# The tail of a Fourier-mixing and GEGLU kernel: the next to last drain copied into buffers of its own ahead of the last chunk's halves, and drain additions spread two per unit

## Chip, cores and metric

The kernel runs on one core of one Trainium2 chip. The metric is the device time of one execution in microseconds (us); the number to compare is the median of several runs. Times inside the program are taken from one profiled execution and counted from the start of its span.

## What is computed

```python
a = jnp.einsum("bsd,ed->bse", x, dft_hid_re)     # x: the input, layer-normed
b = jnp.einsum("bsd,ed->bse", x, dft_hid_im)
y = jnp.einsum("ts,bse->bte", dft_seq_re, a) - jnp.einsum("ts,bse->bte", dft_seq_im, b)
...
h = x + _A_ref(_layernorm(x, axis=-1), ...)      # the mixing above
...
g = jnp.einsum("bsd,df->bsf", x, w_gate)         # x: h, layer-normed
u = jnp.einsum("bsd,df->bsf", x, w_up)
h = _gelu(g) * u
return jnp.einsum("bsf,fd->bsd", h, w_down)
...
h2 = h + _B_ref(_layernorm(h, axis=-1), ...)
```

The sequence has 2048 rows, the model width is 448, the inner width 1792; everything is float32 outside.

## The kernel before

Every float32 operand is split into two float16 halves, a high one (`hi_part`, L108, on ScalarE) and a low one (`lo_part`, L112 or L114, on VectorE, the difference from the high one), and each product is three matrix products of halves. The large products are done by a seven-product scheme on two by two blocks (`STRASSEN`): sums of blocks are formed first, seven products are taken, and the results are sums of products.

The Fourier part takes the first 500 us or so. After it come 42 *units* `t` = 0 to 41, each of which makes one block of gate and up products (`GateUp`: steps `x1`, `z1`, `y1`, `x2`, `z2`, `y2`, `y3`, in PSUM banks X, Y, Z, and others). A unit's weights `gw` are loaded from device memory two units ahead (`gw_load`, L1130) into a ring of three tiles `w0`, `w1`, `w2`; unit t uses tile t mod 3. The hidden values go to device memory and come back as tiles `hid` (`hid_load`, L1137, six buffers).

From unit 14 on the down product runs between the gate and up products. Its rows lie in eight *strips* `p` of 256 rows; a strip is seven *chunks*, so chunk d belongs to strip d // 7. Before a chunk is multiplied, VectorE forms five sums of its blocks (`dn_sums`, L1188 to L1190), ScalarE its high halves (`dn_hi`: one instruction on the raw blocks, one on the sums), VectorE its low halves (`dn_lo`, the same two). A chunk is 21 matrix products in the order of the seven, three each (`dn_mm`, L1218).

A strip's products gather in PSUM banks. Strip 6 uses banks X, tr, Z and Y; strip 7 uses a0 to a3 and, for its sixth product, X. When a strip ends, it is *drained* (`Drain`, L940) into a tile `hr` that holds h: `copy` has ScalarE copy the first two banks to two tiles `v` (L954), `bank2` and `bank3` have VectorE add the other two from PSUM (L958), and `sums` does eight additions (L986) of the copies, then `dn_store` (L1245) sends the strip out. Strips 0 to 4 are drained in the units that follow, with the eight additions on VectorE, three at the end of each unit; strips 5 and 6 are drained in the tail with the additions on GpSimd. Strip 7 ends the program: the last three chunks, 53 to 55, are multiplied product by product, and VectorE adds each finished product to the result (L1498).

The work is ordered by hand: each engine runs its instructions in the order in which this program issues them. All transfers are issued from one queue, SP, in program order; a transfer that has to wait holds those behind it. In a unit the hid loads come first, then `gw_load(t + 2)`, then a load of `hr` where one is due, then the store of hid; a strip's `dn_store` stands at the end of a unit.

The tail (L1462 on) multiplies chunks 42 to 52 (i = 0 to 10). Some chunks have been split in the units (`EARLY`: 42 to 46 and 49 to 51), the others, `jit` = 47, 48, 52, 53, 54, 55, are split in the tail, one behind each chunk's products. Their buffers are few: chunk 54 takes that of chunk 48.

Of the kernel before, what the change touches and what calls it, by code (L numbers as in the profile page):

```python
# [9 lines left out]
F32 = mybir.dt.float32  # L10
# [3 lines left out]
P = 128  # L14
S, D, DF = 2048, 448, 1792
# [17 lines left out]
def kernel(  # L33
# [40 lines left out]
    V, A, G, PE = nc.vector, nc.scalar, nc.gpsimd, nc.tensor  # L74
# [4 lines left out]
    ring = ctx.enter_context(tc.tile_pool(name="ring", bufs=2))  # L79
# [27 lines left out]
    def hi_part(dst, src, scale=1.0):  # L107
        A.activation(dst, src, AF.Copy, scale=scale)  # L108

    def lo_part(dst, src, hi, scale=1.0):  # L110
        if isinstance(scale, float) and scale == 1.0:
            V.tensor_sub(dst, src, hi)  # L112
        else:
            V.scalar_tensor_tensor(dst, src, scale, hi, op0=ALU.mult, op1=ALU.subtract)  # L114
# [293 lines left out]
    def step_of(n):  # L408

        k, qq = divmod(n - NT, 4)  # L410
        return 2 + k // 2, k % 2, qq
# [420 lines left out]
    for n in range(N_STEPS):  # L832
# [78 lines left out]
        else:  # L911
            p, part, qq = step_of(n)
# [25 lines left out]
    fpool = ctx.enter_context(tc.tile_pool(name="fpool", bufs=1, side="right", reuse_waits="tile"))  # L938
# [191 lines left out]
    def gw_load(t):  # L1130
        gw[t] = w_tile(f"gw{t}", t % 3)
        nc.sync.dma_start(gw[t], w_dram[f_of(t)])
# [4 lines left out]
    def hid_load(d):  # L1137
        p, n = divmod(d, NC)
        hid_in[d] = fpool.tile([P, 4, P], F32, tag="hid", bufs=6, name=f"hid{d}")
        b = max(p // 2 - 1, 0)  # L1140
        nc.sync.dma_start(hid_in[d], hid_dram[b, n][:, p % 2 if b else p])

    def dn_hid(d):
        return hid_in[d]
# [17 lines left out]
    def dn_tile(d):  # L1162
        if d in homes:
            make, k, n = homes[d]
            if k == 0:
                opened[make] = make()
            w = opened[make][:, k * n : (k + 1) * n]
        elif d % 5 < 3:
            w = fpool.tile([P, 14 * P], F16, tag="dn_w", bufs=3, name=f"dn_w{d}")
        else:  # L1170
            w = prep.tile([P, 14 * P], F16, tag="raw", bufs=2, name=f"dn_w{d}")
        return w.rearrange("p (l a t) -> p l a t", l=2, a=7)

    def dn_sums(d):
        t = dn_hid(d)
        if d in LAST:
            spare.append(d)
            s = fops.tile([P, 5, P], F32, tag=("xn", "tt")[len(spare) % 2], name=f"dn_s{d}")
        elif d % 4 < 2:
            if d % 4 == 0:  # L1180
                opened["l"] = late.tile([P, 10, P], F32, tag="dn_s", name=f"dn_s{d}")
            s = opened["l"][:, d % 4 * 5 :][:, :5]
        else:
            if d % 4 == 2:
                opened["s"] = prep.tile([P, 10, P], F32, tag="s", name=f"dn_s{d}")
            s = opened["s"][:, d % 4 % 2 * 5 :][:, :5]
        dn_s[d] = s
        V.tensor_add(s[:, 0:2], t[:, 0:2], t[:, 2:4])  # L1188
        V.tensor_sub(s[:, 2:4], t[:, 1:4:2], t[:, 0:4:2])
        V.tensor_add(s[:, 4], t[:, 0], t[:, 3])  # L1190

    def dn_parts(d):
        return (dn_hid(d)[:, 0:4:3], slice(0, 2)), (dn_s[d], slice(2, 7))

    def dn_hi(d):
        dn_w[d] = dn_tile(d)
        for src, dst in dn_parts(d):
            hi_part(dn_w[d][:, 0, dst], src)

    def dn_lo(d):  # L1200
        for src, dst in dn_parts(d):
            lo_part(dn_w[d][:, 1, dst], src, dn_w[d][:, 0, dst])
# [15 lines left out]
    def dn_mm(d, products=range(21)):  # L1218
        p, n = divmod(d, NC)
        if n == 0 and 0 in products:  # L1220
            dn_banks(p)
        w = dn_w[d]
        for i in products:
            k, m = divmod(i, 3)
            a, b = STRASSEN[k]
            la, lb = ((0, 0), (0, 1), (1, 0))[m]
            ps, opens = acc_d[p, "sums"][k]
            PE.matmul(  # L1228
                ps,
                w[:, la, a, :],  # L1230
                wd[n][:, lb, b, :],
                start=n == 0 and m == 0 and opens,
                stop=n == NC - 1 and m == 2,
                skip_group_check=True,
            )

    def hr_load(p):
        hr[p] = pair_tile(f"hr{p}", (0, 1, 4)[p % 3] if p < 6 else p - 4)
        nc.sync.dma_start(hr[p], h_dram[p])

    def dn_drain(p):
        v = [fpool.tile([P, D], F32, tag=f"v{k}", bufs=1, name=f"v{k}_{p}") for k in range(2)]
        return Drain(hr[p], acc_d.pop(p), v, 1.0 / (H_SC * W_SC))

    def dn_store(p):  # L1245
        nc.sync.dma_start(outr[p // 4, p % 4], hr[p])
# [4 lines left out]
    def do(t, k):  # L1251
        for what in side.pop((t, k), ()):
            what()
# [47 lines left out]
    for t in range(NF):  # L1301
        w = gu.get(t + 2) if t + 2 in JIT_F else None
        n = PREP_AT.get(t)
# [89 lines left out]
    drains, ended = {}, {}  # L1393
    for t in range(NF, N_GU):
        now, ahead = steps[t], steps.get(t + 1, [])
        split = EARLY.get(t - 1)
        far = steps.get(t + 2, []) + ([EARLY[t + 1]] if t + 1 in EARLY else [])
        far += [47] if t + 1 == N_GU else []
        for d in far + ([52, 53, 54] if t + 1 == N_GU else []):
            hid_load(d)  # L1400
        if t + 2 < N_GU:
            gw_load(t + 2)
        for d in ahead:
            if d % NC == 0:
                hr_load(d // NC)
        if t in (N_GU - 4, N_GU - 2):
            hr_load(6 + (t == N_GU - 2))
        dn_mm(now[0], range(0, 6))
        prev.y3()
        if t % 2 == 0:  # L1410
            prev.store()
        cur.y1()
        if now[0] % NC:
            cur.z1()
        cur.x2()
        dn_mm(now[0], range(6, 13 if len(now) == 1 else 21))
        for d in ahead:
            dn_hi(d)
        if split is not None:
            dn_hi(split)  # L1420
        cur.z2()
        do(t, 1)
        cur.y2()
        for d in ahead[:1]:
            dn_lo(d)
        if len(now) == 1:
            dn_mm(now[0], range(13, 21))
        else:
            dn_mm(now[1])
        ends = now[-1] % NC == NC - 1  # L1430
        ends = ends and t + 1 < N_GU
        if ends:
            p = now[-1] // NC
            ended[p], drains[p] = t, dn_drain(p)
            drains[p].copy((0,))
        prev = cur
        if t + 1 < N_GU:
            cur = GateUp(t + 1)
            cur.x1()
        if ends:  # L1440
            drains[p].copy((1,))
            drains[p].bank2()
            drains[p].bank3()
            cur.z1()
        prev.c_last()
        for d in ahead[1:]:
            dn_lo(d)
        if split is not None and t + 1 < N_GU:
            dn_lo(split)
        for d in far:  # L1450
            dn_sums(d)
        do(t, 2)
        do(t, 3)
        do(t, 4)
        for p, t0 in ended.items():
            n = 3 * (t - t0)
            if p < 5 and 3 <= n <= 9:
                drains[p].sums(range(n - 3, min(n, 8)), V)
            if p < 5 and n == 9:
                dn_store(p)  # L1460

    prev.y3()  # L1462
    hid_in[48], hid_in[55] = [hs[N_GU - 1][:, 4 * k : 4 * k + 4] for k in range(2)]
    jit = (47, 48, 52, 53, 54, 55, None)
    dn_lo(EARLY[N_GU - 2])
    for i, d in enumerate(range(6 * NC, 7 * NC + 4)):
        dn_mm(d)
        if i < 6:
            dn_hi(jit[i])
            dn_lo(jit[i])  # L1470
            if jit[i + 1]:
                dn_sums(jit[i + 1])
        if i == 3:
            drains[5] = dn_drain(5)
            drains[5].copy()
            drains[5].bank2()
            drains[5].bank3()
        if i == 4:
            drains[5].sums(range(8))
            dn_store(5)  # L1480
        if i == NC - 1:
            drain = dn_drain(6)
            drain.copy()
            drain.bank2()
            drain.bank3()
        if i == NC + 1:
            drain.sums(range(8))
            dn_store(6)
# [73 lines left out]
```

## Time and profile before

| | us |
|---|---|
| median of three runs | 710.6 (709.39 to 711.34) |
| the profiled execution | 710.66 |
| its span, first to last instruction | 708.89 |
| TensorE busy | 699.8 (99%) |
| VectorE busy | 539.1 (76%) |
| ScalarE busy | 395.4 (56%) |
| GpSimd busy | 93.8 (13%) |

In the profile PE is TensorE's matrix products, PEld its weight loads, DVE is VectorE, ACT ScalarE, POOL GpSimd and SPq the queue that issues transfers. A timeline row has the start, the time from the first start to the last end of the merged instructions, the engine, the line, the operation, what it writes and reads, how many instructions were merged, and in brackets how long the engine stood still before and what ended that. A waits row has who waited for whom, the total, the number of times and the longest. A windows row has a stretch, its length, the busy time of engines with their instruction counts in parentheses, the granted TensorE clock, the share of the DMA engines and GB/s. A landing is the time from a transfer's issue to its arrival.

### The profile page before, as it was taken

The numbers are of one execution on the slowest core, as the hardware profiler recorded it, in microseconds if no ns is written. First come the engines' busy times: TensorE is split into PE (matmuls) and PEld (weight loads), VectorE is DVE, ScalarE is ACT, GpSimd is POOL, SyncE is SP. The second block draws the span as 40 slices with busy tenths as digits, with TensorE's granted clock in tenths as the row PEclk, the third lists the DMA queues.
The fourth block names the chain that finished last, engine by engine and source line by source line (L and its number), as shares of the span: only waits on it lengthen the run. The fifth ranks groups of instructions, "written<-read, shape, count | busy, mean of one in ns | idle before, by whom it ended". The sixth has DMA issues, their size and how long they took to land.

```text
span 708.9 us, 13463 instructions
## 1 busy us (share of the span) xinstructions
PE 699.8 (99%) x5092; PEld 493.8 (70%) x5092; DVE 539.1 (76%) x1164; ACT 395.4 (56%) x778; POOL 93.8 (13%) x88
## 2 busy tenths in 40 slices
PE   9999999999999999999999999999999999999987
PEld 5555555555555698897644444479999999998987
DVE  7997647685968879796548789667778686989883
ACT  5776647566575755655437566454645544556530
POOL 0000000000000000000313333411211111331232
PEclk9999999999999999999999999999999999999998
DMA  8788569999999457376836767797869986868601
GB/s 272 251 257 307 119 207 233 298 303 250 297 291 320 118 148 183 116 189 212 227 120 248 260 233 211 191 354 241 253 182 330 241 289 203 328 187 323 228 28 53
DMA packets 116321, 161.29 MB, mean 228 GB/s; under 512 B 61984, under 2 KB 80544, under 8 KB 116256
## 3 DMA queue, kind: packets, MB, share of 16 engines
q1 hardware_dynamic: 116256, 160.43, 74.0%
q8 instruction: 40, 0.66, 0.4%
q14 instruction: 25, 0.20, 0.1%
HBM read 112.16 MB, written 34.34 MB: 207 GB/s over the span
## 4 chain that ended last, share of the span: by engine, by line
PE 97%; issue 1%; ACT 1%; DMA 1%; DVE 0%; ACTq 0%; SPq 0%
PE acc L637 28%; PE acc_d L1228 15%; PE pY L1024 14%; PE acc_f L509 11%; PE pX L1024 9%; PE pZ L1024 9%; PE y L719 9%; DMA wr<-in_w_seq_dram 1%; ACT dn_w L108 0%; DVE dn_w L112 0%; ACTq L1558 0%; ACT v L954 0%; ACT ws L108 0%; SPq L360 0%; DVE hr L1498 0%
## 5 line engine op out<-in xcount | busy, mean ns | idle before, releaser
L637 PE MATMUL acc<-xs,ws 128*128 128x448 f16 x1056 | 201.2, 353 | 0.2 <-ACT ws L108 0.2
L1024 PEld LDWEIGHTS <-gw 128*128 128x128 f16 x1443 | 140.6, 98 | 53.1 <-DMA gw<-w_dram 1.3
L637 PEld LDWEIGHTS <-ws 128*128 128x128 f16 x1056 | 103.0, 98 | 96.9 <-ACT ws L108 0.4
L1228 PE MATMUL acc_d<-wd,dn_w 128*128 128x224 f16 x1008 | 110.7, 260 | 0.0
L1228 PEld LDWEIGHTS <-dn_w 128*128 128x128 f16 x1008 | 96.8, 98 | 2.1
L1024 PE MATMUL pY<-hops,gw 128*128 128x256 f16 (+1 forms) x629 | 98.1, 299 | 0.0
L114 DVE SCALAR_TENSOR_TENSOR ws<-wr,ws 128x1024 f16<-128x1024 f32 (+2 forms) x66 | 73.0, 1109 | 26.3 <-ACT ws L108 25.7
L1118 POOL TENSOR_TENSOR hs<-hs,c 128x256 f32<-128x256 f32 (+1 forms) x42 | 59.3, 1412 | 247.7 <-ACT c L1116 181.4
L509 PEld LDWEIGHTS <-ws 128*128 128x128 f16 x840 | 80.5, 98 | 1.3
L1024 PE MATMUL pX<-hops,gw 128*128 128x256 f16 (+1 forms) x407 | 67.1, 299 | 1.0 <-ACT v L954 1.0
L108 ACT ACTIVATE ws<-wr 128x1024 f16<-128x1024 f32 (+2 forms) x66 | 62.8, 954 | 9.0 <-DMA wr<-in_w_seq_dram 6.8
L1024 PE MATMUL pZ<-hops,gw 128*128 128x256 f16 (+1 forms) x407 | 67.1, 299 | 0.0
L719 PE MATMUL y<-wh,z 128*128 128x448 f16 x336 | 66.2, 353 | 0.0
L509 PE MATMUL acc_f<-t,ws 128*128 128x224 f16 x480 | 57.0, 260 | 0.0
L1069 ACT ACTIVATE pY<-pX 128x256 f32<-128x256 f32 (+1 forms) x42 | 18.4, 439 | 67.4 <-PE pX L1024 63.9
L215 POOL TENSOR_TENSOR wd_s<-wd 128x448 f32<-128x448 f32 x7 | 9.6, 1366 | 340.4 <-DMA gu_raw<-in_w_gu_dram 339.6
L719 PEld LDWEIGHTS <-z 128*128 128x128 f16 x336 | 32.8, 98 | 29.7
L1080 ACT ACTIVATE u<-pY 128x256 f32<-128x256 f32 (+1 forms) x42 | 19.1, 454 | 53.6 <-PE pY L1024 53.4
L1034 DVE SCALAR_TENSOR_TENSOR c<-pZ,u 128x256 f32<-128x256 f32 (+1 forms) x42 | 21.4, 510 | 35.2 <-PE pZ L1024 21.9
L509 PE MATMUL acc_f<-xs,ws 128*128 128x224 f16 x360 | 45.6, 260 | 0.0
L112 DVE TENSOR_TENSOR dn_w<-dn_s,dn_w 128x640 f16<-128x640 f32 x48 | 41.8, 872 | 1.9 <-ACT dn_w L108 1.9
L108 ACT ACTIVATE dn_w<-dn_s 128x640 f16<-128x640 f32 x48 | 34.9, 728 | 11.4 <-DVE dn_s L1190 11.4
(144 smaller groups left out, 890.7 us busy)
## 6 DMA issues: line engine op xcount, KB each, us to landing
gw<-w_dram SPq DMA_DIRECT2D x37, 896.0 KB, 6.3
wr<-in_w_seq_dram SPq DMA_DIRECT2D x100, 256.0 KB, 4.5
hid_dram<-hs SPq DMA_DIRECT2D x27, 512.0 KB, 5.5
hid<-hid_dram SPq DMA_DIRECT2D x54, 256.0 KB, 5.3
w_dram<-gu_w SPq DMA_DIRECT2D x14, 896.0 KB, 6.0
gu_raw<-in_w_gu_dram SPq DMA_DIRECT2D x28, 384.0 KB, 5.8
wr<-in_w_seq_dram SPq DMA_DIRECT2D x14, 512.0 KB, 5.4
x<-in_x_dram SPq DMA_DIRECT2D x16, 224.0 KB, 3.0
```

What stands on the lines that cost most here:

```text
L108: A.activation(dst, src, AF.Copy, scale=scale)
L112: V.tensor_sub(dst, src, hi)
L114: V.scalar_tensor_tensor(dst, src, scale, hi, op0=ALU.mult, op1=ALU.subtract)
L509: PE.matmul(fast_sum(n, k), fast_a(n, i, lw, a), fast_b(j, lx, b), start=j == 0 and m == 0 and k % 2 == 0, stop=j == NT // 2 - 1 and m == ...
L637: PE.matmul(acc[key][:, :D], w[:, lw, block * P : (block + 1) * P], xs[c][:, lx, :], start=c == 0 and m == 0, stop=c == NT - 1 and m == 2,)
L719: PE.matmul(y[:, :D], z[p][:, lz, k, g * P : (g + 1) * P], wh[:, lw, k, :], start=p == NP - 1 and k == 0 and m == 0, stop=k == 6 and m == ...
L1024: PE.matmul(ps, w[:, wl, wa + ws, :], ops[:, m + ms, :], start=first and n == 0, stop=last and n == len(terms) - 1, skip_group_check=True,)
L1034: V.scalar_tensor_tensor(dst, ps, SC, other, op0=ALU.mult, op1=ALU.add)
L1069: A.activation(self.Y, self.X, AF.Copy)
L1080: A.activation(self.u2, self.Y, AF.Copy, scale=SC)
L1118: G.tensor_mul(c22, c22, self.cols(self.c12))
L1228: PE.matmul(ps, w[:, la, a, :], wd[n][:, lb, b, :], start=n == 0 and m == 0 and opens, stop=n == NC - 1 and m == 2, skip_group_check=True,)
```

## The change

Three edits. Drain 6 takes its two copies in a tile of the weight ring (`w0`) instead of the two tiles `v0`, `v1` that the other drains share. In the tail the split of chunk 55 moves from behind chunk 47 (i = 5) to behind drain 6's copies and bank additions (i = 6). The additions of drains 3 and 4 are done two at the end of each unit over four units, instead of three over three; so their stores stand one unit later.

```diff
     def dn_drain(p):
-        v = [fpool.tile([P, D], F32, tag=f"v{k}", bufs=1, name=f"v{k}_{p}") for k in range(2)]
+        if p == 6:
+            v = ring.tile([P, 4, D], F32, tag="w0", bufs=1, name=f"v_{p}")
+            v = [v[:, 0], v[:, 1]]
+        else:
+            v = [fpool.tile([P, D], F32, tag=f"v{k}", bufs=1, name=f"v{k}_{p}") for k in range(2)]
         return Drain(hr[p], acc_d.pop(p), v, 1.0 / (H_SC * W_SC))
...
         for p, t0 in ended.items():
-            n = 3 * (t - t0)
-            if p < 5 and 3 <= n <= 9:
-                drains[p].sums(range(n - 3, min(n, 8)), V)
-            if p < 5 and n == 9:
+            each = 3 if p < 3 else 2
+            n = each * (t - t0)
+            if p < 5 and 0 < n < 8 + each:
+                drains[p].sums(range(n - each, min(n, 8)), V)
+            if p < 5 and 8 <= n < 8 + each:
                 dn_store(p)
...
-    jit = (47, 48, 52, 53, 54, 55, None)
+    jit = (47, 48, 52, 53, 54, 55)
...
-        if i < 6:
+        if i < 5:
             dn_hi(jit[i])
             dn_lo(jit[i])
-            if jit[i + 1]:
-                dn_sums(jit[i + 1])
+            dn_sums(jit[i + 1])
...
             drain.copy()
             drain.bank2()
             drain.bank3()
+            dn_hi(jit[5])
+            dn_lo(jit[5])
```

ScalarE at the end of the program, before: `dn_w54` and `dn_w55` are the halves of chunks 54 and 55, `v0_6` and `v1_6` the copies of drain 6.

```order
L954 ACTIVATE v1_5_8438<-acc_d5_1_7864 128x448
L108 ACTIVATE dn_w54_8466<-hid54_8209 128x256
L108 ACTIVATE dn_w54_8466<-dn_s54_8433 128x640
L108 ACTIVATE dn_w55_8505<-hs_40_8156 128x256
L108 ACTIVATE dn_w55_8505<-dn_s55_8471 128x640
L954 ACTIVATE v0_6_8531<-acc_d6_0_8313 128x448
L954 ACTIVATE v1_6_8532<-acc_d6_1_8314 128x448
```

The same place of the changed kernel, where `v_6` is the tile of the ring:

```order
L954 ACTIVATE v1_5_8438<-acc_d5_1_7864 128x448
L108 ACTIVATE dn_w54_8466<-hid54_8206 128x256
L108 ACTIVATE dn_w54_8466<-dn_s54_8433 128x640
L954 ACTIVATE v_6_8526<-acc_d6_0_8313 128x448
L954 ACTIVATE v_6_8526<-acc_d6_1_8314 128x448
L108 ACTIVATE dn_w55_8533<-hs_40_8154 128x256
L108 ACTIVATE dn_w55_8533<-dn_s55_8471 128x640
```

The two copies have moved ahead of the two instructions of chunk 55.

VectorE at the same place, before: the low halves of chunk 54, the sums of chunk 55 (`dn_s55`), its low halves, and drain 6's additions from PSUM into `hr6`.

```order
L112 TENSOR_TENSOR dn_w54_8466<-dn_s54_8433,dn_w54_8466 128x640
L1188 TENSOR_TENSOR dn_s55_8471<-hs_40_8156 128x256
L1189 TENSOR_TENSOR dn_s55_8471<-hs_40_8156 128x256
L1190 TENSOR_TENSOR dn_s55_8471<-hs_40_8156 128x128
L112 TENSOR_TENSOR dn_w55_8505<-hs_40_8156,dn_w55_8505 128x256
L112 TENSOR_TENSOR dn_w55_8505<-dn_s55_8471,dn_w55_8505 128x640
L958 SCALAR_TENSOR_TENSOR hr6_7861<-acc_d6_2_8315,hr6_7861 128x224 x3
L958 SCALAR_TENSOR_TENSOR hr6_7861<-acc_d6_3_8316,hr6_7861 128x224
```

And now:

```order
L112 TENSOR_TENSOR dn_w54_8466<-dn_s54_8433,dn_w54_8466 128x640
L1188 TENSOR_TENSOR dn_s55_8471<-hs_40_8154 128x256
L1189 TENSOR_TENSOR dn_s55_8471<-hs_40_8154 128x256
L1190 TENSOR_TENSOR dn_s55_8471<-hs_40_8154 128x128
L958 SCALAR_TENSOR_TENSOR hr6_7861<-acc_d6_2_8315,hr6_7861 128x224 x3
L958 SCALAR_TENSOR_TENSOR hr6_7861<-acc_d6_3_8316,hr6_7861 128x224
L112 TENSOR_TENSOR dn_w55_8533<-hs_40_8154,dn_w55_8533 128x256
L112 TENSOR_TENSOR dn_w55_8533<-dn_s55_8471,dn_w55_8533 128x640
```

The four additions of drain 6 have moved ahead of the low halves of chunk 55.

The queue SP from the end of unit 35 to unit 37, before: `out_0_dram<-hr3` is the store of strip 3, `gw38` the weights of unit 38.

```order
L1132 DMA gw37_7502<-w_dram11_156 128x3584
L1246 DMA out_0_dram<-hr3_6592 128x2x448
L1141 DMA hid35_7605<-hid_dram1_0_3974 128x512
L1141 DMA hid36_7607<-hid_dram1_1_3975 128x512
L1141 DMA hid51_7609<-hid_dram2_2_3983 128x512
L1132 DMA gw38_7611<-w_dram5_150 128x3584
L1128 DMA hid_dram2_3_3984<-hs_34_7440 128x1024
L1141 DMA hid37_7733<-hid_dram1_2_3976 128x512
L1141 DMA hid45_7735<-hid_dram2_3_3984 128x512
L1132 DMA gw39_7737<-w_dram12_157 128x3584
L1239 DMA hr5_7739<-h_dram5_142 128x896
```

And now:

```order
L1132 DMA gw37_7500<-w_dram11_156 128x3584
L1141 DMA hid35_7602<-hid_dram1_0_3974 128x512
L1141 DMA hid36_7604<-hid_dram1_1_3975 128x512
L1141 DMA hid51_7606<-hid_dram2_2_3983 128x512
L1132 DMA gw38_7608<-w_dram5_150 128x3584
L1128 DMA hid_dram2_3_3984<-hs_34_7439 128x1024
L1250 DMA out_0_dram<-hr3_6592 128x2x448
L1141 DMA hid37_7733<-hid_dram1_2_3976 128x512
L1141 DMA hid45_7735<-hid_dram2_3_3984 128x512
L1132 DMA gw39_7737<-w_dram12_157 128x3584
L1239 DMA hr5_7739<-h_dram5_142 128x896
```

The store of strip 3 has moved behind unit 36's three hid loads, the load of gw38 and the store of hid. Likewise the store of strip 4 has moved behind the four hid loads of unit 41. PE's instructions are the same in both kernels, in the same order.

## Prediction

> **What bounds the kernel now.** I read the page first, then what TensorE (PE) and its weight loads (PEld) waited for, then the timeline around each wait.
>
> ```profile
> span 708.9 us, 13463 instructions
> PE 699.8 (99%) x5092; PEld 493.8 (70%) x5092; DVE 539.1 (76%) x1164; ACT 395.4 (56%) x778; POOL 93.8 (13%) x88
> ```
> ```profile
> PE acc_d L1228 <- ACT v L954: 3.3, 1, 3.3
> PE pX L1024 <- ACT v L954: 1.0, 1, 1.0
> ```
> PE is busy for 99% of the span and the change leaves its instructions and their order alone. So only time in which PE stands still, or runs at a lower clock, can be won. These are its two waits after the start-up; both name the drain's copy.
>
> *The long one*, in the tail, PE's timeline:
>
> ```profile
> 672.55 4.19 PE L1228 MATMUL acc_d<-wd,hops 128*128 128x224 f16 x42
> 676.58 4.19 PE L1228 MATMUL acc_d<-wd,dn_l 128*128 128x224 f16 x42
> ...
> 686.64 1.60 PE L1228 MATMUL acc_d<-wd,hops 128*128 128x224 f16 x15
> 691.57 1.28 PE L1228 MATMUL acc_d<-wd,hops 128*128 128x224 f16 x6 [3.33 <-ACT v L954]
> 692.64 3.03 PE L1228 MATMUL acc_d<-wd,dn_l 128*128 128x224 f16 x21
> 695.50 2.18 PE L1228 MATMUL acc_d<-wd,dn_xs 128*128 128x224 f16 x21
> ```
> Undisturbed, 42 products take 676.58 - 672.55 = 4.03 us from start to start, 0.096 us each. The 42 products of chunks 49 and 50 (15 + 6 + 21) take 695.50 - 686.64 = 8.86 us. They lose **4.83 us** in two parts: the 16th product could start at 686.64 + 15 x 0.096 = 688.08 and starts at 691.57 (3.49 us); the 27 after it take 3.93 us and not 2.59 (1.34 us). The windows view shows the second part as a clock:
>
> ```profile
> 690.60:691.60 1.00, 0.03 (x1) 0.69 0.33 124
> 691.60:692.60 1.00, 1.00 (x6) 0.50 0.00 0
> ```
> The third number from the end is the granted clock. A mean of 0.69 puts the fall from 1 to a half at about 691.0, some 2.8 us after PE came to stand.
>
> The 16th product is the first that writes bank X, which drain 6's first copy must have read. ScalarE (ACT) at that time:
>
> ```profile
> 686.89 0.42 ACT L108 ACTIVATE dn_w<-hid 128x256 f16<-128x256 f32 x1 [3.99 <-issue]
> 687.21 0.72 ACT L108 ACTIVATE dn_w<-dn_s 128x640 f16<-128x640 f32 x1
> 687.84 0.40 ACT L108 ACTIVATE dn_w<-hs 128x256 f16<-128x256 f32 x1
> 690.35 0.74 ACT L108 ACTIVATE dn_w<-dn_s 128x640 f16<-128x640 f32 x1 [2.11 <-DVE dn_s L1190]
> 690.99 0.96 ACT L954 ACTIVATE v<-acc_d 128x448 f32<-128x448 f32 x2
> ```
> Chunk 54's two halves, chunk 55's two, then the copies. Chunk 54 is held until chunk 48's products end (its buffer is theirs); chunk 55's second half waits 2.11 us for VectorE's (DVE) sums, and the copies stand behind it.
>
> *The short one* is not the copy's, though the view says so:
>
> ```profile
> 638.94 0.93 PE L1228 MATMUL acc_d<-wd,dn_w 128*128 128x224 f16 x8
> 640.88 0.83 PE L1024 MATMUL pX<-hops,gw 128*128 128x256 f16 x6 [1.01 <-ACT v L954]
> ```
> ```profile
> PEld L1024 <- DMA gw<-w_dram: 1.3, 1, 1.3
> ```
> ```profile
> 631.12 0.39 SPq L1246 DMA_DIRECT2D out_dram<-hr  x1
> ...
> 633.35 0.42 SPq L1132 DMA_DIRECT2D gw<-w_dram  x1
> ```
> ```profile
> gw<-w_dram SPq DMA_DIRECT2D x1, 896.0 KB, 7.5
> ```
> The product is unit 38's first and reads weights gw38. Their load was issued at 633.35 and took 7.5 us: it landed at 640.85, and PE began at 640.88. The copy that ended then touches no bank of pX. PE could have begun at 638.94 + 8 x 0.096 = 639.71, so this stop costs **1.17 us**. The load was late because strip 3's store (631.12) stood ahead of it and waited for DVE's last additions.
>
> **The change, part by part.**
>
> *The copies go ahead of chunk 55's halves, into a buffer of their own.* They now follow chunk 54's halves, so the first starts where chunk 55's started, 687.84. A copy is 0.53 us (two in 0.96), and PE began 0.05 us after one ended (690.99 + 0.53 against 691.57). So PE goes on at 687.84 + 0.58 = 688.42, against 688.08: a stop of 0.34 us for 3.49. The buffer is the weight ring's w0, last read by the first products of unit 40; it brings no wait. In the old pair, the first copy would have to wait for GpSimd's (POOL) second of four additions of drain 5, at about 685.96 + 1.4 = 687.4, and so not at all; the second for the fourth, at 688.8, half a us:
>
> ```profile
> 685.96 2.80 POOL L986 TENSOR_TENSOR hr<-hr,v 128x224 f32<-128x224 f32 x4 [0.29 <-DVE hr L958]
> ```
> PE waits for the first alone, so the order brings the gain and the buffer next to nothing.
>
> *The clock.* Does a stop of 0.34 us lose it? The 1.01 us stop at 640 did not:
>
> ```profile
> 640.00:641.00 1.00, 0.12 (x2) 0.11 (x2) 1.00 (x4) 0.88 (x2) 0.00 (x0) 1.00 0.98 398
> 641.00:642.00 1.00, 1.00 (x11) 0.90 (x10) 0.97 (x3) 0.26 (x1) 0.00 (x0) 1.00 0.64 246
> ```
> The granted clock, third from the end, is 1.00 in that stop and behind it, so I take the 1.34 us as won too. Tail: 4.83 - 0.34 = **4.49 us**. [...]
>
> *What is queued behind the copies.* Chunk 55's halves on ACT (0.96 us later at worst) and its two low halves on DVE, which now follow drain 6's four additions.
>
> ```profile
> 682.81 0.88 DVE L1188 TENSOR_TENSOR dn_s<-hid 128x256 f32<-128x256 f32 x1
> ...
> 685.08 1.53 DVE L958 SCALAR_TENSOR_TENSOR hr<-acc_d,hr 128x224 f32<-128x224 f32 x4
> ...
> 687.34 0.91 DVE L112 TENSOR_TENSOR dn_w<-hid,dn_w 128x256 f16<-128x256 f32 x1 [0.73 <-ACT dn_w L108]
> 688.17 1.27 DVE L112 TENSOR_TENSOR dn_w<-dn_s,dn_w 128x640 f16<-128x640 f32 x1
> 689.37 0.41 DVE L1188 TENSOR_TENSOR dn_s<-hs 128x256 f32<-128x256 f32 x1
> ```
> POOL's additions of drain 6 now start at about 688.8 and run beside DVE, so chunk 55's three sums take the slow time of chunk 54's (685.08 - 682.81 = 2.27 us), not 0.87: from 689.37 to 691.64. Then the four additions, 1.53, to 693.17, and the low halves at the slow 0.91 and 1.27: 694.1 and 695.3. PE, at 688.42, has 69 products to do before the last stage and reaches chunk 55's first low half after 77 at 688.42 + 77 x 0.096 = 695.8, its second after 95, at 697.5. Both are covered, by 1.7 and 2.2 us; without that cover each us late costs one. Drain 6's store moves no later (POOL ends near 695.9). The end of the program is PE's last product, one addition and a store, and moves with PE.
>
> *Two additions per unit for strips 3 and 4.*
>
> ```profile
> 630.41 0.68 DVE L986 TENSOR_TENSOR hr<-hr,v 128x224 f32<-128x224 f32 x2
> ```
> The same 16 additions; two (0.68 us) move from units 33 to 35 into unit 36, for strip 4 from 38 to 40 into 41. What counts is the queue SP: strip 3's store goes past unit 36's three hid loads, gw38 and the store of hid. The loads then wait for DVE's reads of three chunks, the last this one, and gw38 for PE's old reads:
>
> ```profile
> 627.60 0.41 DVE L112 TENSOR_TENSOR hops<-hid,hops 128x256 f16<-128x256 f32 x1
> ```
> ```profile
> DMA to landing us min/median/max: 4.5/6.4/8.9
> ```
> PE has done those by then (gw35's last reading is unit 36's first matrix work). So hid51 goes at 628.0, gw38 half a us behind, at about 628.5 instead of 633.35, and even with the slowest landing of the thirteen loads that this row counts (8.9 us) is there at 637.4, before 639.71. **1.17 us** won.
>
> The store now waits for DVE in unit 36, with hid37, hid45, gw39 and hr5 queued behind it.
>
> ```profile
> 639.36 0.42 DVE L1103 SCALAR_TENSOR_TENSOR hs<-pY,g 128x256 f32<-128x256 f32 x1
> ```
> ```profile
> DVE dn_s L1188 <- DMA hid<-hid_dram: 1.9, 2, 1.3
> ```
> Unit 36's sums of three chunks ended at 639.36, with 1.9 us of waiting for late hid loads in them. Without that they end near 637.5, the two additions near 638.2, and the store is out then. Behind it hid37 goes at once; hid45 reads what the hid store ahead has written, so I leave 2 us for it, and gw39 is issued near 640.4. Strip 4's store likewise goes behind four hid loads, which can only be earlier for it. Its two additions in unit 41 delay DVE's halves of chunk 46 by 0.68 us; PE comes to them only after the 84 products of chunks 42 to 45 (8 us by the tail's first rows), so I cost them at nothing.
>
> **Sum.** 4.49 + 1.17 = 5.66 us. The profiled execution took 710.66 (span 708.89 and 1.8 around it): 710.66 - 5.66 = **705.0 us**. It stood 0.06 above the median of 710.6, so no correction.
>
> **Rivals.** *The short stop comes back at another load.* PE reaches the first work of units 39 and 41 1.17 us earlier.
>
> ```profile
> 649.34 0.66 PE pX L1024 x6
> ```
> For unit 39 that is 649.34 - 1.17 = 648.2 and leaves gw39 648.2 - 640.4 = 7.8 us, more than the median landing and less than the slowest. And gw41 had little to spare:
>
> ```profile
> 657.71 0.38 SPq L1132 DMA_DIRECT2D gw<-w_dram  x1
> ```
> ```profile
> gw<-w_dram SPq DMA_DIRECT2D x1, 896.0 KB, 5.1
> ```
> ```profile
> 663.72 0.82 PE L1024 MATMUL pX<-hops,gw 128*128 128x256 f16 x6
> ```
> It landed at 662.81 for 663.72. It is queued behind a hid load that waits for a store of DVE's and POOL's results. For it: that chain is long. Against it: DVE is freed of 1.9 us of waits. At most the 1.17 is lost: 710.66 - 4.49 = 706.2. Chance 0.16.
>
> *The half clock is not this stop's*: it falls anyway, for some other cause. Then 710.66 - 5.66 + 1.34 = 706.3. The trace shows it once only, and inside the stop; 0.07. [...]
>
> *The copies stay late*, held by something that no row shows, and gw38 too: 710.7, no change; 0.05.
>
> *Slower: strip 3's store blocks SP.* Its place is the end of unit 36; PE needs gw39 at 648.2. A stop there of S us, with the clock lost too, costs S + 1.34: it eats the gain at S = 4.3 and is slower by over 0.3% (2.1 us) from S = 6.5, gw39 landing at 654.7. Eight us late give 705.0 + 9.3 = 714.3. It needs DVE to end unit 36 some 8 us later than worked out; no row speaks for that. 0.03.
>
> **Numbers.** 0.3% (2.1 us) is about what a measurement of this kernel can tell from no change; its three runs spread from 709.39 to 711.34, 1.2 below and 0.7 above the median. The forecast has 0.69 (705.0; 704.7 if the remaining 0.34 is hidden too). Down: 704.7 and a run's 1.2, 703.4. Up: the second rival and 0.7, 707.0. All three cases in that range are faster: 0.92; same 0.05; slower 0.03.
>
> **What would show it.** Right: PE's wait for the copy some 0.3 us, no window under 1.00 around 688 to 695, ACT's copies directly behind chunk 54's halves, gw38 issued near 628.5 and no wait in x1 of unit 38. Wrong: a wait of PE on gw39 or gw41, on chunk 55's halves after the copies, or a half clock in the tail all the same.

## The result, and the profile after

| | before | after |
|---|---|---|
| median | 710.69 us (709.39 to 711.34, 6 runs) | 705.91 us (705.51 to 707.5, 6 runs) |
| ratio, 95% interval | | 0.9938 [0.9924, 0.9952] |
| profiled execution | 710.66 | 706.23 |
| its span | 708.89 | 704.46 |

The change makes the kernel faster by 4.8 us. 705.0 was forecast, so the time is 0.9 above the forecast and inside its range. A second measurement (below) gave 705.72 against 711.47.

The page of the changed kernel: PE still fills 99% of the span, and its clock row shows 90% or more in every slice, where before's last slice was lower.

```profile
span 704.5 us, 13462 instructions
...
PE 699.3 (99%) x5092; PEld 494.0 (70%) x5092; DVE 536.5 (76%) x1164; ACT 394.7 (56%) x778; POOL 97.3 (14%) x88
```

What PE waits for in the changed kernel. The wait for the copy is 0.2 us instead of 3.3, and the wait in pX, unit 38's, is gone. The 0.5 is new in this view; it lies at 469 us, far from the change, and is taken up under "why".

```profile
PE acc_d L1228 <- DVE dn_w L112: 0.5, 1, 0.5
PE acc_d L1228 <- ACT v L954: 0.2, 1, 0.2
```

PE's timeline in the tail of the changed kernel, chunks 49 and 50 (15 + 6 + 21 products) and what follows:

```profile
686.73 1.60 PE L1228 MATMUL acc_d<-wd,hops 128*128 128x224 f16 x15
688.51 0.73 PE L1228 MATMUL acc_d<-wd,hops 128*128 128x224 f16 x6 [0.17 <-ACT v L954]
689.08 2.17 PE L1228 MATMUL acc_d<-wd,dn_l 128*128 128x224 f16 x21
691.09 2.18 PE L1228 MATMUL acc_d<-wd,dn_xs 128*128 128x224 f16 x21
693.10 7.06 PE L1228 MATMUL acc_d<-wd,dn_w 128*128 128x224 f16 x72
```

The 42 products take 691.09 - 686.73 = 4.36 us; before they took 8.86. So the tail won 4.50 us. In the same two stretches in which the clock had been 0.69 and 0.50, it is now 1.00 (third number from the end):

```profile
690.60:691.60 1.00, 1.00 (x13) 1.00 0.41 156
691.60:692.60 1.00, 1.00 (x13) 1.00 0.00 0
```

ScalarE in the changed kernel: the copies follow chunk 54's halves without a gap, and only chunk 55's second half waits for VectorE, with nothing behind it.

```profile
687.30 0.72 ACT L108 ACTIVATE dn_w<-dn_s 128x640 f16<-128x640 f32 x1
687.93 0.95 ACT L954 ACTIVATE v<-acc_d 128x448 f32<-128x448 f32 x2
688.78 0.41 ACT L108 ACTIVATE dn_w<-hs 128x256 f16<-128x256 f32 x1
691.82 0.74 ACT L108 ACTIVATE dn_w<-dn_s 128x640 f16<-128x640 f32 x1 [2.63 <-DVE dn_s L1190]
```

VectorE and GpSimd there. Chunk 55's sums run from 689.45 at the slow pace (the first took 0.88 us with GpSimd at work, 0.41 in before with GpSimd standing still), then drain 6's four additions, then the two low halves, ready by 693.6 and 694.8; PE comes to the first of them 77 products after 688.51, at about 695.9.

```profile
689.45 0.88 DVE L1188 TENSOR_TENSOR dn_s<-hs 128x256 f32<-128x256 f32 x1
...
691.72 1.52 DVE L958 SCALAR_TENSOR_TENSOR hr<-acc_d,hr 128x224 f32<-128x224 f32 x4
693.16 0.41 DVE L112 TENSOR_TENSOR dn_w<-hs,dn_w 128x256 f16<-128x256 f32 x1
693.49 1.28 DVE L112 TENSOR_TENSOR dn_w<-dn_s,dn_w 128x640 f16<-128x640 f32 x1
```
```profile
686.05 6.26 POOL L986 TENSOR_TENSOR hr<-hr,v 128x224 f32<-128x224 f32 x8 [0.29 <-DVE hr L958]
692.60 3.30 POOL L986 TENSOR_TENSOR hr<-hr,v 128x224 f32<-128x224 f32 x4 [0.28 <-DVE hr L958]
```

The queue SP around unit 36 in the changed kernel: three hid loads, gw38, the store of hid, and only then strip 3's store, which waits until 638.83 with gw39 behind it.

```profile
626.72 2.99 SPq L1141 DMA_DIRECT2D hid<-hid_dram  x3
629.80 0.38 SPq L1132 DMA_DIRECT2D gw<-w_dram  x1
632.85 0.32 SPq L1128 DMA_DIRECT2D hid_dram<-hs  x1
638.83 0.39 SPq L1250 DMA_DIRECT2D out_dram<-hr  x1
...
640.59 0.43 SPq L1132 DMA_DIRECT2D gw<-w_dram  x1
```

PE where unit 38 begins: its first product follows the eight before it with no wait in brackets.

```profile
640.22 0.93 PE L1228 MATMUL acc_d<-wd,dn_w 128*128 128x224 f16 x8
640.98 0.82 PE L1024 MATMUL pX<-hops,gw 128*128 128x256 f16 x6
```

From the start of the eight to the start of the six it is 0.76 us, before 640.88 - 638.94 = 1.94: 1.18 us won.

So two stretches won 4.50 + 1.18 = 5.68 us by the traces, while the spans differ by 708.89 - 704.46 = 4.43. The row at 640.22 stood at 638.94 before: the changed kernel's profiled execution came to unit 38 1.28 us *late*, through code that the change does not touch. Whether that is a cost of the change or chance is one of the questions for the experiments.

### The profile page after: what moved, and what is told of

Its sections match the earlier page's. It is cut to its first block, busy times and chain, and to the rows that moved or that the text cites. A ratio compares the mean times of both kernels' runs of the same rounds, so it can differ in the third digit from the quotient of the medians.

```text
span 704.5 us, 13462 instructions
## 1 busy us (share of the span) xinstructions
PE 699.3 (99%) x5092; PEld 494.0 (70%) x5092; DVE 536.5 (76%) x1164; ACT 394.7 (56%) x778; POOL 97.3 (14%) x88
## 4 chain that ended last, share of the span: by engine, by line
PE 96%; DMA 1%; DVE 1%; issue 1%; SPq 1%; ACT 0%; POOL 0%; POOLq 0%; DVEq 0%
PE acc L637 28%; PE acc_d L1228 15%; PE pY L1024 14%; PE acc_f L509 11%; PE y L719 9%; PE pX L1024 9%; PE pZ L1024 9%; DMA hid_dram<-hs 1%; PE pw L102 1%; SPq L1141 0%; DVE wd L114 0%; SPq L294 0%; DVE xs L112 0%; ACT dn_w L108 0%; ACT v L954 0%
## 5 line engine op out<-in xcount | busy, mean ns | idle before, releaser
L1118 POOL TENSOR_TENSOR hs<-hs,c 128x256 f32<-128x256 f32 (+1 forms) x42 | 62.1, 1478 | 246.7 <-ACT c L1116 168.9
```

Source lines behind the costliest of these rows:

```text
L1118: G.tensor_mul(c22, c22, self.cols(self.c12))
```

## Experiments

The theory: the order of the copies brings the tail's gain, clock included; the place of strip 3's store in SP brings unit 38's; the buffer and strip 4 bring nothing. Rivals: the buffer is what lets the copies go early; the freed VectorE, not the queue, ends unit 38's stop; the half clock has another cause.

PE's 5092 products stand in the same order in all kernels, so each trace can be laid on that of before product by product, both counted from the start of their spans. The table gives how much later (+) or earlier (-) a run's trace is than before's: when it enters unit 38's neighbourhood (the 4400th product), what unit 38 adds, and what the 42 products of the tail add (with three instructions ahead of the copies, up to the end of the half clock, which outlasts the 42).

| run | median us | ratio | at product 4400 | unit 38 | tail |
|---|---|---|---|---|---|
| the change | 705.91 | 0.9938 [0.9924, 0.9952] | +1.28 | -1.18 | -4.51 |
| order alone | 706.64 | 0.9932 [0.9914, 0.9951] | +0.34 | +0.22 | -4.51 |
| buffer alone | 711.45 | 0.9997 [0.9985, 1.0009] | +0.78 | -0.47 | +0.29 |
| additions alone | 709.86 | 0.9976 [0.9963, 0.9989] | +0.92 | -1.18 | +0.30 |
| stores alone | 710.29 | 0.9978 [0.9965, 0.9990] | +0.34 | -1.18 | -1.37 |
| copies ahead of 54 too | 704.88 | 0.9919 [0.9902, 0.9935] | +1.01 | -1.18 | -4.84 |
| the same, old buffer | 705.53 | 0.9926 [0.9908, 0.9943] | +0.66 | -1.18 | -4.84 |
| change, 2 instructions ahead of the copies | 707.01 | 0.9948 [0.9932, 0.9964] | +0.06 | -1.18 | -2.69 |
| change, 3 of them | 709.58 | 0.9974 [0.9963, 0.9985] | +0.12 | -1.18 | -0.04 |
| the change again | 705.72 | 0.9914 [0.9895, 0.9933] | +2.10 | -1.18 | -4.51 |
| strip 3 alone in twos | 705.83 | 0.9918 [0.9900, 0.9936] | +0.52 | -1.18 | -4.51 |
| copies ahead of 54 again | 705.19 | 0.9908 [0.9891, 0.9925] | +1.19 | -1.18 | -4.84 |

The kernel before had 711.48 beside the runs in rows two to five, 711.33 beside the next four, 711.47 beside the last three.

**Order alone.** Of the change only the tail's order; `v0`, `v1` and the additions as before.

```diff
-    jit = (47, 48, 52, 53, 54, 55, None)
+    jit = (47, 48, 52, 53, 54, 55)
...
-        if i < 6:
+        if i < 5:
...
             drain.bank3()
+            dn_hi(jit[5])
+            dn_lo(jit[5])
```

> Chunk 55's split behind drain 6's copies, but the copies still in the old pair of tiles and the additions three per unit. If the order alone brings the tail's gain: the first copy starts as in the full change, PE's stop in the tail is some 0.3 us, the clock keeps 1.00 there, the stop at unit 38 stays: about 4.5 us faster than before, near 706.2. If the buffer of its own is needed: the copies wait for GpSimd's last addition of drain 5, PE's stop is 1.2 us or more, near 707.

706.64 against 711.48. The tail wins 4.51 us, as much as with the whole change. ScalarE and PE in this kernel:

```profile
688.40 0.53 ACT L954 ACTIVATE v<-acc_d 128x448 f32<-128x448 f32 x1
689.35 0.54 ACT L954 ACTIVATE v<-acc_d 128x448 f32<-128x448 f32 x1 [0.42 <-POOL hr L986]
```
```profile
688.98 0.73 PE L1228 MATMUL acc_d<-wd,hops 128*128 128x224 f16 x6 [0.17 <-ACT v L954]
```

The first copy is not held, the second is, 0.42 us, by GpSimd's additions of drain 5 that still read `v1`; PE goes on after the first. Unit 38's stop stays, and PE's waits now name its cause, where before's view named a copy that only ended at the same moment:

```profile
PE pX L1024 <- DMA gw<-w_dram: 1.2, 1, 1.2
```

**Buffer alone.** Drain 6 copies into the ring tile, in the old order.

```diff
+        if p == 6:
+            v = ring.tile([P, 4, D], F32, tag="w0", bufs=1, name=f"v_{p}")
+            v = [v[:, 0], v[:, 1]]
```

> Only the buffer of its own. If the order is what counts: the copies still stand behind chunk 55's second half, the stop of 3.3 us and the half clock stay, time as before, 710.7 within 0.5. If the wait for the old buffer was the cause: 3 us or more faster.

711.45 against 711.48, the same time; PE's stop for the copy is still 3.3 us. The buffer alone brings nothing.

**Additions alone.** The two additions per unit for strips 3 and 4, tail as before.

```diff
+            each = 3 if p < 3 else 2
+            n = each * (t - t0)
```

> Only the two additions per unit for strips 3 and 4. Theory: PE's stop at unit 38 (1.0 us by the profile, 1.17 from start to start) goes, the tail's stop stays: about 1.2 us faster, 709.5. Rival (the stop moves to another load): time as before, with a wait of PE on gw39 or gw41.

709.86: 1.6 us won, with an interval from 0.8 to 2.6. In the trace unit 38's stop is gone (1.18) and the tail keeps its own.

**Stores alone.** Three additions per unit as before; only the stores of strips 3 and 4 stand one unit later.

```diff
-            if p < 5 and n == 9:
+            if p < 5 and n == (9 if p < 3 else 12):
```

> Three additions per unit as before, but the stores of strips 3 and 4 one unit later, where the change has them. If the store's place in the queue SP was what held gw38: gw38 is issued some 5 us earlier than before, the stop at unit 38 goes, about 1.2 us faster, 709.5. If VectorE's fewer additions in units 33 to 35 were needed: the stop stays, 710.7.

710.29: the same 1.18 us at unit 38. gw38 is issued at 628.78 and strip 3's store behind it:

```profile
628.78 0.38 SPq L1132 DMA_DIRECT2D gw<-w_dram  x1
632.04 0.32 SPq L1128 DMA_DIRECT2D hid_dram<-hs  x1
632.41 0.43 SPq L1246 DMA_DIRECT2D out_dram<-hr  x1
```

VectorE's additions are where they were, so it is the store's place in the queue that ends the stop; the spreading of the additions is not needed for it. This trace also holds a surprise: the tail's stop is there in full, and no clock is lost behind it.

```profile
690.72 0.73 PE L1228 MATMUL acc_d<-wd,hops 128*128 128x224 f16 x6 [3.31 <-ACT v L954]
691.29 2.18 PE L1228 MATMUL acc_d<-wd,dn_l 128*128 128x224 f16 x21
693.30 2.18 PE L1228 MATMUL acc_d<-wd,dn_xs 128*128 128x224 f16 x21
```

The 27 products take 693.30 - 690.72 = 2.58 us, at full clock; before they took 3.93 after a stop of 3.33. The profiled runs of "buffer alone" and "additions alone", with stops of 3.31 and 3.32 us, lost it. Nor is it this one execution: of the twelve of this kernel, four have a mean granted clock of 0.999 or 1.000 and took 708.46 to 708.86, and eight have 0.997 or 0.998 and took 710.13 to 711.57 (what such a mean tells is worked out under "why").

**Copies ahead of chunk 54 too.** The remaining stop: the copies need nothing of chunk 54's halves, which wait for chunk 48's products.

```diff
-        if i < 5:
+        if i < 4:
...
             drain.copy()
+            dn_hi(jit[4])
+            dn_lo(jit[4])
+            dn_sums(jit[5])
             drain.bank2()
```

> The full change, and drain 6's copies also ahead of chunk 54's halves (which wait for the last product of chunk 48; each copy needs only its own bank's products). Theory: the first copy starts some 2.5 us earlier, in ScalarE's idle time, PE's remaining stop in the tail of 0.17 us (0.34 from start to start) goes, nothing else moves: 0.3 us faster than the change, 705.6. Rival (something behind comes later): a new wait of PE on chunk 54 or 55, 706 or more.

704.88. The copies go at 685.23, in what was ScalarE's idle time, and PE runs through:

```profile
685.23 1.12 ACT L954 ACTIVATE v<-acc_d 128x448 f32<-128x448 f32 x2 [2.50 <-PE acc_d L1228]
```
```profile
686.46 2.18 PE L1228 MATMUL acc_d<-wd,hops 128*128 128x224 f16 x21
```

The tail is 0.33 us better than with the change, as worked out for the rest of the stop.

**The same in the old buffer.** Here GpSimd's additions of drain 5 do hold the copies, and chunk 54's and 55's halves stand behind them.

> As the run with the copies ahead of chunk 54's halves, but in the old pair of tiles. Here the buffer should count: the second copy waits for GpSimd's last addition of drain 5, some 2 us behind chunk 48's end, and chunks 54 and 55 stand behind it. PE does not stop at bank X, but waits about 1 us for chunk 55's low half: 706.5 to 707.5. If the buffer counts nowhere: 705.6.

705.53, and the expected wait of PE did not come. The copies are held as expected (4.47, then 0.69 us), but they still end before PE needs the bank, and PE shows no stop:

```profile
686.85 0.54 ACT L954 ACTIVATE v<-acc_d 128x448 f32<-128x448 f32 x1 [4.47 <-POOL hr L986]
688.08 0.54 ACT L954 ACTIVATE v<-acc_d 128x448 f32<-128x448 f32 x1 [0.69 <-POOL hr L986]
```
```profile
686.12 2.18 PE L1228 MATMUL acc_d<-wd,hops 128*128 128x224 f16 x21
```

So the buffer is worth nothing to PE in either order.

**Two and three instructions ahead of the copies.** To the change, a delay of known size: ScalarE instructions that copy weights to where nobody reads them (0.96 us each), ahead of drain 6's copies.

```diff
+            for _ in range(2):
+                A.activation(pads[0], wd[0][:, 0, 0:4].rearrange("p a d -> p (a d)"), AF.Copy)
             drain.copy()
```

> The full change with two instructions of ScalarE that copy constant weights into the unused half of the drain's tile, ahead of drain 6's copies, about 0.86 us each. Nothing is left out. PE's stop in the tail becomes about 2.0 us. If a stop costs its length alone: 1.7 us slower than the change, 707.6. If the half clock comes with it, 1.3 us more: 708.9.

> As the run before with three such instructions: stop about 2.9 us. At its length alone 2.6 us slower than the change, 708.5; with the half clock as in the kernel before, which stood 3.3 us, 709.8.

With two, PE stops for 2.00 us and keeps the clock: the tail loses 4.51 - 2.69 = 1.82 us, the stop alone (2.00 - 0.17 = 1.83).

```profile
689.11 0.73 PE L1228 MATMUL acc_d<-wd,hops 128*128 128x224 f16 x6 [2.00 <-ACT v L954]
689.68 2.18 PE L1228 MATMUL acc_d<-wd,dn_l 128*128 128x224 f16 x21
```

With three, PE stops for 2.98 us and the clock falls, 1.3 us after PE is at work again:

```profile
690.16 0.74 PE L1228 MATMUL acc_d<-wd,hops 128*128 128x224 f16 x6 [2.98 <-ACT v L954]
690.73 3.40 PE L1228 MATMUL acc_d<-wd,dn_l 128*128 128x224 f16 x21
693.92 2.65 PE L1228 MATMUL acc_d<-wd,dn_xs 128*128 128x224 f16 x21
```
```profile
691.00:692.00 1.00, 1.00 (x10) 0.74 0.00 0
692.00:693.00 1.00, 1.00 (x8) 0.50 0.00 0
...
694.00:695.00 1.00, 1.00 (x8) 0.55 0.00 0
```

The tail gives back 4.47 of its 4.51 us: 2.81 of the stop and 1.66 of the clock. So the half clock is this stop's; with 2.00 us of stop it is gone, with 2.98 it is back. That its length alone does not decide, the run with the stores alone has shown; the last section takes it up.

**The change, strip 3 alone, and copies ahead of 54, side by side.** The change once more; with strip 4 back to three additions per unit (`each = 2 if p == 3 else 3`); and the better order once more.

> The changed kernel once more, beside the two others on one chip. If the span lost nothing by the change and only the profiled execution of before was a lucky one, as the theory has it (tail 4.5 and unit 38 1.2), the median is 5.0 to 5.7 below before's, a ratio of 0.992 to 0.993. The rival, that the change really brings only 4.5 to 4.8 as the medians of the result have it, expects 0.9933 to 0.9937 again.

> The change, but only strip 3 takes its additions in twos; strip 4 takes them in threes as before. The prediction cost strip 4's part at nothing: then no wait at units 38 to 41 comes back, the unit 38 stop stays away, and the time is that of the change within 0.3. Rival: strip 4's store, one unit earlier again, holds the load of unit 42's time or a hid load behind it, and PE stops at unit 41 or in the first chunks of the tail by up to 1 us.

> The change with drain 6's copies also ahead of chunk 54's halves, once more, beside the change itself. Theory: the change's remaining stop of 0.17 seen by the profile, 0.33 by the starts of the products, goes and nothing else moves: 0.3 us below the change, ratio of the two near 0.9995. Rival: the 1.0 us between the two medians so far (704.88 against 705.91) is real, and it is 1.0 below again.

705.72, 705.83 and 705.19 against 711.47. The change is 5.75 us below before here, a shade more than its traces' 5.69; the interval, 4.8 to 7.5 us, holds the forecast's 5.66, which the first measurement's (3.4 to 5.4) just missed. Strip 4's part makes 0.11 us, nothing. The better order is 0.53 us below the change, between the 0.3 of the theory and the 1.0 of the rival; the traces say 0.33 again, and the medians of six runs that spread over 1.4 to 2.1 us cannot settle the rest. It is the fastest version tried.

## Why the prediction was right

*PE's stops are all there is to win.* Right. Beside the two stretches named only waits moved that come and go between executions (see below).

*The tail's stop, 3.49 for 0.34, by order.* Right to 0.02 us: 4.50 by the rows, 4.51 product by product, 4.49 forecast. The order alone brings all of it.

*The clock, 1.34.* Right in cause: the rival that it has another cause fell with the run of three added instructions, where a stop of 2.98 us brought the half clock back. It was not a constant, though: the run with the stores alone had the same stop and lost no clock. The term belongs to most executions of before, not to all. An estimate: a half clock of 3.4 us, as the four traces that have it show (3.40 to 3.42), takes 0.5 x 3.4 / 709 = 0.0024 off the mean clock of an execution, so one with a mean of 0.999 or 1.000 has not had it. Of the 57 executions of before beside the experiments nine have such a mean, and took 709.51 to 710.13; the other 48 have 0.998 or less, and their median is 711.7. The mean does not say where in the program the clock fell; only the traces do.

*The buffer brings next to nothing.* Right: 0.9997 alone, and no stop of PE without it. The second copy's wait that it spares was forecast at half a us and measured at 0.42.

*The queue, 1.17.* Right: 1.18 in every kernel in which the store stands behind gw38, and the run with the stores alone shows that it is the queue. gw38 was issued at 629.80 for 628.5; that trace was 1.28 us late at this place, so the step itself was on time. The stop did not come back at another load: PE's waits show none.

*Chunk 55's halves are covered.* Right: ready by 693.6 and 694.8, forecast 694.1 and 695.3. The three sums took the slow time forecast, 2.27 us to the start of what follows them (691.72 - 689.45). The first low half took 0.41 us and not the slow 0.91; why, the rows do not show, since GpSimd was at work beside it.

*Strip 4 costs nothing.* Right: 705.72 with its additions in twos, 705.83 with them in threes.

*"It stood 0.06 above the median, so no correction."* This step failed, and it is where most of the 0.9 us lie. The median of three runs was itself low: beside the later runs the kernel before had 711.3 to 711.5, from which the forecast would have been 705.7 to 705.8. And the profiled execution of before was a quick one in code that the change does not touch: at the 4400th product the twelve other traces stand 0.06 to 2.10 us behind it, eight of them by more than 0.5. In the changed kernel's trace two places make 1.0 of its 1.28 us. One is the start, PE's 44 transposes, in before and in the changed kernel, 0.38 us by the first product behind them:

```profile
1.37 4.29 PE L102 MATMUL pw<-ident 128*128 128x128 f16 x44 [1.37 <-POOL sign_t L93]
```
```profile
1.37 4.88 PE L102 MATMUL pw<-ident 128*128 128x128 f16 x44 [1.37 <-POOL sign_t L93]
```

The other is unit 14, 0.61 us, where VectorE waits for a store of hid to be out, before and after, and in the changed kernel PE then stops for VectorE's half:

```profile
466.97 0.69 DVE L1034 SCALAR_TENSOR_TENSOR hs<-pY,m 128x512 f32<-128x512 f32 x1 [0.74 <-DMA hid_dram<-hs]
```
```profile
467.99 0.69 DVE L1034 SCALAR_TENSOR_TENSOR hs<-pY,m 128x512 f32<-128x512 f32 x1 [1.34 <-DMA hid_dram<-hs]
```
```profile
469.07 0.56 PE L1228 MATMUL acc_d<-wd,dn_w 128*128 128x224 f16 x4 [0.46 <-DVE dn_w L112]
```

That this is chance and no cost of the change is borne out by the runs of the table that have the change's units up to 37: they range from +2.10 (the change itself, again) to +0.06 (the change with two instructions added), and those with before's own units stand at +0.34 and +0.78. The gain of the two stretches was right; the base that it was taken from was up to 0.9 us low. Why the six runs of before beside the result kept to 710.69 stays open: no clock of theirs is on record. So its gain of 4.8 us and the second measurement's 5.75 stand side by side.

## What to carry to other kernels

When a copy frees a bank that the bottleneck engine is about to write, put it ahead of everything on its engine that waits for someone else: here four instructions in another order brought 4.5 us, and a buffer of its own brought nothing. In a queue that issues in order, a store that waits for late work holds every load behind it (gw38 was issued at 633.35 behind strip 3's store and at 628.78 ahead of it, which was worth 1.18 us): move the store behind the loads that are due, not the work. And lay several traces of a kernel on each other before taking one as the base of a sum: what a single profiled execution gains or loses in untouched code can be as large as a term.

## What the runs showed of the hardware

The half clock was not a matter of the stop's length alone: PE stood for 3.31 us with the stores alone and kept the clock, and for 2.98 us with three instructions ahead of the copies and lost it. The half clock lasted 3.40 to 3.42 us in each of the four traces that have it; its ends are worked out from the rows of the granted clock in which it is neither 1.00 nor 0.50, taking it to be one or the other. In the run of three instructions it goes from 691.48 (0.74 in its first row above) to 694.90 (0.55 in its last). In before it fell at about 690.98 (0.69 from 690.60 on, in the prediction's rows), inside the stop; in the other cases 0.15 to 1.32 us after PE was back at work:

| run | PE stood still | us | half clock |
|---|---|---|---|
| before | 688.24 to 691.57 | 3.33 | 690.98 to 694.38 |
| additions alone | 687.98 to 691.30 | 3.32 | 692.06 to 695.48 |
| buffer alone | 688.56 to 691.87 | 3.31 | 692.02 to 695.44 |
| three instructions | 687.18 to 690.16 | 2.98 | 691.48 to 694.90 |
| stores alone | 687.41 to 690.72 | 3.31 | none, 1.00 in all rows from 690.60 to 694.60 |
| two instructions | 687.11 to 689.11 | 2.00 | none, 1.00 in all rows from 686.00 to 695.00 |

Behind PE's last product the clock falls once more; in before at about 708.03, 2.30 us after that product's end (0.52, third number from the end):

```profile
708.00:708.80 0.80, 0.00 (x0) 0.52 0.00 0
```

What beside its length decides whether a stop costs the clock was not shown. How often the clock was kept can be estimated from the lists of runs: of the 93 executions of the four kernels whose traces have a stop of 3.31 to 3.33 us, 17, or 0.18, have a mean clock of 0.999 or 1.000.

The cost was 1.34 us where part of the half clock fell into the stop (before), and 1.66 where all of it fell on work (three instructions).
